# A fused Mamba-2 and SwiGLU kernel: two more value products in three parts, and a new order of the steps

## The chip, the core and the metric

The kernel runs on one core of a Trainium2 chip. The core has TensorE (PE, matrix products, with PEld loading its weights), VectorE (DVE), ScalarE (ACT), GpSimd (POOL) and SyncE (SP, which here issues nearly all transfers). Each engine has a queue of its own and runs it in order; an instruction waits by semaphores for what it needs. Products are written to PSUM, which has eight banks; all else lies in SBUF.

The metric is the device time of one execution in microseconds (us). Where a time is named below without more, it is the median of several runs.

## What is computed

A chunked state-space block (Mamba-2 SSD) with 4 batches x 8 heads, 768 tokens, head size 32 and state size 16, and behind it a SwiGLU block on the 3072 tokens with width 256 and 1536 hidden columns:

```python
# per chunk of tokens, per head
cum = np.cumsum(log_a)
L = np.exp(cum[i] - cum[j]) * (i >= j)
y = (C @ B.T * L) @ x + (C @ state) * np.exp(cum)
state = np.exp(sum(log_a)) * state + sum_j(B[j] x[j] * exp(cum[-1] - cum[j]))
# then, on x = y of all heads side by side, 3072 x 256
xn = x / np.sqrt(np.mean(x * x, -1) + 1e-6) * rms_g
g, val = xn @ w_gate, xn @ w_val          # 256 x 1536 each
out = (g / (1 + np.exp(-g)) * val) @ w_out
```

All inputs and outputs are float32.

## The kernel before

**Blocks and tiles.** The tokens are cut into 6 blocks of 512 (number blk), each of two pairs p of 256 tokens, each pair of two chunks g. The hidden columns are cut into 12 tiles f of 128. A gate product (m = 0) or value product (m = 1) of a block and a tile is one 128 x 512 result in one PSUM bank.

**Two ways to multiply.** A float32 product can be done whole (`gv_whole`, L1149, and `o_whole`): two instructions over the two halves of the 256 inner columns, which the trace shows as four records. Or it can be done in three parts (`gv_split`, L1159, and `o_split`, `product_apart`): x and w are each cut into a high part, a low part and a mixed part of the type fp32r, and six instructions add up their products. The parts have to be made first. For x these are `x_high` (the step xH on ScalarE or xHv on VectorE) and `x_part` (xL and xK on VectorE); for a weight piece k, wH or wHv, wL and wM; for a hidden tile, hH or hHv, hL (VectorE) or hLp (GpSimd), and hK. The set `GV4` holds the gate and value products that are done whole, `O4` the output products. Block 0's tiles 0 and 1 are done in another way ("early", L1112).

**Weights.** The weights come in 18 pieces, fetched by transfers (fetch), and are rebuilt from 16-bit words: ScalarE makes a power of two (pow, two instructions), VectorE a mantissa (man), and VectorE joins them (wt). Pieces 2 to 11 hold gate (even) and value (odd) columns, so the value columns of tiles 4 and 5 are piece 5; pieces 12 to 17 are the output weights.

**Order.** Nothing is scheduled by the framework. The text `order` (L1390 to L1516) lists 1200 steps, and the loop below it emits their instructions one after the other; so the text fixes the order in the queue of every engine. A step is a group (i, p or b: settings and first work, pairs, blocks), a kind and numbers. `b:X.1.10.0` is the product in three parts for block 1, tile 10, gate; `b:F.0.4.1` the whole product for block 0, tile 4, value; `b:OF` and `b:OX` are output products (whole, in parts) into one of a block's two result banks; `b:OY` are those of the last block's second half. `b:silu` (ScalarE) takes a gate product out of its bank into hx and frees the bank; `b:hid` (VectorE, L1174) multiplies the value product into hx and frees that bank.

**The state-space steps.** gb makes C B^T for a block (four banks), L multiplies it with the decays, A and S are the states, yi and ya the outputs y. The decays of a chunk are fetched (spread), the token's sum is subtracted (sub on VectorE, subp on GpSimd), the exponential taken (ex, ScalarE) and the upper triangle cut (ca on GpSimd, cav on VectorE). sq and sqa or sqav (GpSimd or VectorE), ms, rs, rb and xn are the norm. ScalarE holds one table of functions at a time: Silu has one, Exp and Ln share another, and a step that needs the other one loads it first (L264, L266; also the steps table and exps).

**Buffers.** `Ring` hands out places first in, first out: eight PSUM banks (`one`), and SBUF places h (512 columns), q, k, s and d. A step that takes a place waits for the last reader of the place that was freed longest ago.

Of the kernel before, what the change touches and what calls it, by code (L numbers as in the profile page):

```python
# [50 lines left out]
def kernel(  # L51
# [1264 lines left out]
    def token_out():  # L1316
# [98 lines left out]
        b:X.0.2.1 i:man.15 i:wH.5 i:man.14 b:table.5 b:hid.0.7 b:X.0.3.1 b:ms.1 i:fetch.17 p:qb.4  # L1415
        i:pow.11 i:pow.15 i:wM.8 i:man.11 i:wL.8 b:X.0.6.1 b:rs.1 b:hid.0.3 p:subp.10 b:X.0.9.0
        b:hid.0.5 b:X.0.8.0 i:pow.13 i:wt.11 i:wt.14 b:hid.0.6 i:pow.9 i:man.9 i:wt.15 i:man.13
        i:pow.17 p:sub.9 i:wHv.11 b:hid.0.2 i:wM.11 i:wt.9 i:wL.11 p:vB.4 p:ex.9 b:OF.0.4.0 i:man.17
        i:wH.9 i:wH.15 p:vC.4 b:OF.0.4.1 i:wt.13 b:OF.0.7.1 i:wL.9 i:wH.13 p:spread.8 b:OF.0.5.1
        i:wM.9 p:Tt.4.0 p:subp.11 p:qb.5 p:vC.5 b:rb.1 p:ex.11 b:X.0.10.0 p:x.4 i:wt.17 p:sub.8  # L1420
# [12 lines left out]
        b:OF.0.11.0 p:scale.7 p:vC.9 i:wL.4 p:scale.6 p:Tt.6.0 b:silu.1.11 b:X.1.1.0 b:table.4
        b:sq.2.1 b:put.0.0 b:hK.1.10 b:X.1.6.0 p:Tt.9.0 b:X.1.11.1 i:wL.15 b:hLp.1.0 i:wM.16
        b:X.1.6.1 b:silu.1.1 b:sq.2.0 b:hK.1.0 b:sqav.2 p:vB.6 p:dT.7 p:spread.12 b:yt.2.0 i:wM.5
        p:spread.13 b:ms.2 b:silu.1.6 i:wM.13 p:A.6 i:wL.16 p:spread.15 p:A.7 p:S.6 b:X.1.5.0
        i:wL.13 b:rs.2 b:hid.1.11 p:Tt.7.0 p:qb.10 i:wL.5 p:scale.9 p:S.7 b:exps.4 b:silu.1.5
        b:X.1.9.1 p:sub.13 b:X.1.1.1 b:X.1.4.0 b:X.1.8.1 b:exps.5 b:rb.2 b:hH.1.11 b:silu.1.4
# [6 lines left out]
        b:X.1.7.1 b:xH.2.0 b:OX.1.8.0 i:wL.14 b:X.1.3.1 b:hHv.1.4 p:yi.7 p:ya.7 p:vB.9 b:xK.2.0
        b:hK.1.1 b:xL.2.0 b:xL.2.1 b:hid.1.3 b:hH.1.2 b:hLp.1.1 b:xK.2.1 b:hLp.1.4 b:hid.1.7
        b:yt.3.0 b:hK.1.4 b:OX.1.8.1 b:hHv.1.9 b:hLp.1.6 b:X.2.2.0 b:hH.1.7 b:OX.1.1.0 p:spread.16
        b:sq.3.1 b:OX.1.4.1 b:hK.1.9 b:OX.1.4.0 b:sq.3.0 p:spread.18 p:vC.8 b:OX.1.1.1 p:x.9
        b:yt.3.1 p:dT.8 b:hL.1.2 b:hLp.1.7 b:X.2.9.0 b:sqav.3 b:hL.1.9 p:qb.8 b:X.2.0.1 b:hK.1.7
        b:X.2.2.1 b:silu.2.2 p:Tt.8.0 b:silu.2.9 p:sub.16 p:scale.11 p:vB.8 b:X.2.11.0 b:OX.1.7.0  # L1450
        p:sub.18 b:OX.1.7.1 p:x.8 b:hH.1.3 b:hK.1.2 p:scale.8 b:OX.1.9.0 b:ms.3 p:A.8 b:OX.1.2.0
        b:hK.1.3 p:S.8 b:hid.2.2 p:spread.17 b:hL.1.3 p:vC.11 p:ex.16 p:subp.17 b:X.2.7.0 b:X.2.5.0
        b:silu.2.11 b:hHv.1.5 p:Tt.8.1 p:Td.8 b:hK.1.6 p:cav.16 p:spread.19 b:X.2.0.0 b:hL.1.5
        b:X.2.5.1 b:silu.2.0 b:OX.1.9.1 b:silu.2.5 p:vB.10 p:qc.10 b:OX.1.3.1 b:hid.2.5 b:rs.3
        p:dT.11 p:qb.11 b:hH.2.5 b:hid.2.0 p:ex.17 p:ex.18 b:X.2.8.0 p:subp.19 b:hK.1.5 p:ca.18
        p:Tt.11.1 b:X.2.11.1 p:dT.9 b:OX.1.6.1 b:hLp.2.5 p:ex.19 b:X.2.4.0 b:rb.3 b:OX.1.6.0
# [98 lines left out]
```

## Time and profile before

| | us |
|---|---|
| median of 3 runs | 364.84 (364.15 to 364.86) |
| the profiled execution | 364.29 |
| its span, first to last instruction | 362.5 |
| TensorE busy | 356.3 |
| VectorE busy | 275.3 |
| ScalarE busy | 183.9 |
| GpSimd busy | 74.8 |

Where the output products of the blocks and the three parts of the gate and value products stand among the costliest groups:

```profile
L1159 PE MATMUL gv<-xh,wh 128*128 128x512 f32 x264 | 84.8, 402 | 0.0
L1159 PE MATMUL gv<-xl,wp 128*128 128x512 f32 x264 | 81.5, 390 | 0.0
L1159 PE MATMUL gv<-xk,wp 128*128 128x512 f32 x264 | 81.4, 389 | 0.0
```

Such a row gives the line, the engine, the operation, what is written and read, the shapes and the count; then the busy time of the group in us and the mean length of one in ns; then the idle time of the engine just ahead of the group's instructions and what ended it. Products overlap in TensorE, so the mean length of a record is more than the step from one to the next. A row of the timeline or of the chain begins with the start and the length in us, counted from the first instruction. A row of waits names the engine, what it was about to do, whom it waited for, the total in us, the number and the longest. "issue" is time for which the trace shows no cause.

### The profile page before, as it was taken

How to read it: one execution, taken by the hardware profiler on the slowest of the kernel's cores; microseconds unless marked ns; L12 is line 12 of the kernel's file. 1: busy time of each engine (PE TensorE's matmuls, PEld its weight loads, DVE VectorE, ACT ScalarE, POOL GpSimd, SP SyncE). 2: the span in 40 equal slices, each digit the busy share in tenths (PEclk: the TensorE clock that was granted, in tenths of full speed). 3: DMA queues.
4: the chain of work that ended last, by engine and by line, in shares of the span. 5: the costliest groups of instructions: out<-in, count | busy, mean ns of one | idle time of the engine just before them, and what ended most of it. 6: DMA issues, size and time to landing. Idle time of an engine off the chain costs nothing.

```text
span 362.5 us, 8200 instructions
## 1 busy us (share of the span) xinstructions
PE 356.3 (98%) x3301; PEld 284.0 (78%) x3301; DVE 275.3 (76%) x514; ACT 183.9 (51%) x323; POOL 74.8 (21%) x79
## 2 busy tenths in 40 slices
PE   8999989999999999999999999999999999999996
PEld 5667467888787888788788788788788888888886
DVE  6899998999999999872787884696457446629591
ACT  3879878697288946563236755225811121231110
POOL 4022004124011036212102626010010000511140
PEclk9999999999999999999999999999999999999999
DMA  8889968367525224423302031200101000100004
GB/s 103 187 140 288 272 193 224 107 151 117 103 85 137 44 40 103 103 54 85 60 12 81 7 88 31 45 0 4 36 0 31 1 0 2 29 0 2 0 7 110
DMA packets 94702, 27.95 MB, mean 77 GB/s; under 512 B 77545, under 2 KB 92617, under 8 KB 94665
## 3 DMA queue, kind: packets, MB, share of 16 engines
q1 hardware_dynamic: 92584, 27.30, 32.8%
q8 instruction: 26, 0.43, 0.5%
q10 hardware_dynamic: 2080, 0.13, 0.4%
q14 instruction: 12, 0.09, 0.1%
HBM read 23.68 MB, written 3.74 MB: 76 GB/s over the span
## 4 chain that ended last, share of the span: by engine, by line
PE 95%; DVE 2%; issue 1%; POOL 1%; ACT 0%; POOLq 0%; DVEq 0%
PE gv L1159 50%; PE o L1228 18%; PE o L1234 7%; PE gv L1149 4%; PE y L916 3%; PE o L1206 2%; PE gv L1112 2%; PE g L765 2%; PE A L830 1%; PE g L758 1%; PE y L891 1%; PE e L609 1%; POOL hl L1080 1%; PE ms L1014 0%; DVE hk L1082 0%
## 5 line engine op out<-in xcount | busy, mean ns | idle before, releaser
L1159 PE MATMUL gv<-xh,wh 128*128 128x512 f32 x264 | 84.8, 402 | 0.0
L1159 PE MATMUL gv<-xl,wp 128*128 128x512 f32 x264 | 81.5, 390 | 0.0
L1159 PE MATMUL gv<-xk,wp 128*128 128x512 f32 x264 | 81.4, 389 | 0.0
L272 ACT ACTIVATE hx<-gv 128x512 f32<-128x512 f32 x70 | 40.1, 595 | 75.3 <-PE gv L1159 36.5
L1080 POOL TENSOR_TENSOR hl<-hx,hh 128x512 fp32r<-128x512 f32 x27 | 39.5, 1473 | 172.4 <-PE o L1228 105.8
L1174 DVE SCALAR_TENSOR_TENSOR hx<-gv,hx 128x512 f32<-128x512 f32 x70 | 46.6, 683 | 26.9 <-PE gv L1159 19.3
L1159 PEld LDWEIGHTS gv<-xl,wp 128*128 128x128 f32 x264 | 49.6, 188 | 10.6
L1159 PEld LDWEIGHTS gv<-xk,wp 128*128 128x128 f32 x264 | 49.6, 188 | 10.6
L1159 PEld LDWEIGHTS gv<-xh,wh 128*128 128x128 f32 x264 | 48.6, 188 | 10.5 <-issue 0.6
L1082 DVE SCALAR_TENSOR_TENSOR hk<-hx,hh 128x512 fp32r<-128x512 f32 x60 | 47.1, 792 | 8.9 <-PE o L1228 6.0
L328 ACT ACTIVATE hh<-hx 128x512 fp32r<-128x512 f32 x35 | 21.8, 629 | 43.2 <-PE o L1228 20.3
L1228 PE MATMUL o<-hh,wh 128*128 128x512 f32 x96 | 38.0, 396 | 0.0
L1228 PE MATMUL o<-hl,wp 128*128 128x512 f32 x96 | 37.4, 390 | 0.0
L1228 PE MATMUL o<-hk,wp 128*128 128x512 f32 x96 | 37.4, 389 | 0.0
L1080 DVE TENSOR_TENSOR hl<-hx,hh 128x512 fp32r<-128x512 f32 x33 | 24.1, 744 | 5.3 <-PE o L1228 3.7
L631 POOL TENSOR_SCALAR_AFFINE_SELECT L<-L 64x512 f32<-64x512 f32 (+1 forms) x22 | 18.7, 851 | 45.8 <-ACT L L272 45.0
L322 DVE SCALAR_TENSOR_TENSOR wp<-wh,w 128x512 fp32r<-128x512 f32 x36 | 26.3, 756 | 1.0 <-ACT wh L328 1.0
L1234 PE MATMUL o<-w,hx 128*128 128x256 f32 x96 | 23.0, 381 | 0.0
L1228 PEld LDWEIGHTS o<-hh,wh 128*128 128x128 f32 x96 | 18.0, 188 | 4.3 <-issue 0.4
L1228 PEld LDWEIGHTS o<-hk,wp 128*128 128x128 f32 x96 | 18.0, 188 | 3.8
L1228 PEld LDWEIGHTS o<-hl,wp 128*128 128x128 f32 x96 | 18.0, 188 | 3.5
L1234 PEld LDWEIGHTS o<-w,hx 128*128 128x128 f32 x96 | 18.0, 189 | 3.4 <-issue 0.4
(180 smaller groups left out, 504.3 us busy)
## 6 DMA issues: line engine op xcount, KB each, us to landing
L<-rowd SPq DMA_DIRECT2D x32, 128.0 KB
x<-in_x_dram SPq DMA_DIRECT2D x24, 128.0 KB
wr<-in_moe_w_out_dram SPq DMA_DIRECT2D x6, 511.5 KB
wr<-in_moe_w_gate_dram SPq DMA_DIRECT2D x5, 511.5 KB
wr<-in_moe_w_val_dram SPq DMA_DIRECT2D x5, 511.5 KB
out_dram<-ob SPq DMA_DIRECT2D x32, 64.0 KB
bc<-in_B_dram SPq DMA_DIRECT2D x23, 64.0 KB
bc<-in_C_dram SPq DMA_DIRECT2D x23, 64.0 KB
```

The costliest lines, as they stand in the source:

```text
L272: nc.scalar.activation(**operands)
L322: nc.vector.scalar_tensor_tensor(out=(low_parts, mixed_parts)[i][k], in0=high_parts[k], scalar=(-UP, GAIN)[i], in1=view(ws[k], shape), op0 ...
L328: nc.scalar.activation(out=out, in_=in_, func=AF.Copy, scale=scale)
L631: nc.gpsimd.affine_select(out=L[r], in_=L[r], pattern=[[0, L.shape[1]], [1, HC]], compare_op=ALU.is_ge, fill=0.0, base=0, channel_multipli ...
L916: nc.tensor.matmul(out=o[first:first + n, (p % 2 * 2 + i) * HC:(p % 2 * 2 + i + 1) * HC], start=not groups & opened, stop=True, skip_group ...
L1080: engine.tensor_tensor(out=out, in0=v, in1=high, op=ALU.subtract)
L1082: nc.vector.scalar_tensor_tensor(out=out, in0=v, scalar=REST, in1=high, op0=ALU.mult, op1=ALU.subtract)
L1149: nc.tensor.matmul(out=o, lhsT=view(ws[k], fetched[k][2])[:, t, f % 2 * P:][:, 0:P], rhs=xn[:, t], start=(t == 0), stop=(t == 1))
L1159: nc.tensor.matmul(out=o, lhsT=weights_of(m, t, f)[part], rhs=view(x, [P, TB], F32R), start=(part == t == 0), stop=(part == 2 and t == 1))
L1174: nc.vector.scalar_tensor_tensor(out=v, in0=o, scalar=gain(blk, f), in1=v, op0=ALU.mult, op1=ALU.mult)
L1228: nc.tensor.matmul(out=o, lhsT=w[:, b * P:(b + 1) * P], rhs=v, start=opens, stop=True, skip_group_check=True)
L1234: nc.tensor.matmul(out=o[:, j * DM:(j + 1) * DM], lhsT=v[:, tk], rhs=w, start=opens, stop=True, skip_group_check=True)
```

## The change

`GV4` loses (0, 4, 1) and (0, 5, 1): the value products of block 0's tiles 4 and 5 are done in three parts. So the steps F.0.4.1 and F.0.5.1 become X.0.4.1 and X.0.5.1. By the functions above, the hidden tiles (0, 4) and (0, 5) get another constant factor in `hid` (`gain`), the places of xH, xL, xK of block 0 and of weight piece 5 get other counts of uses, and nothing else is computed differently.

The first 150 of the 1200 steps stay as they are. All others stand in a new order. In it some steps change their form, which moves them from one engine to another; in all:

| kind | before | after | engine |
|---|---|---|---|
| F / X | 8 / 132 | 6 / 134 | TensorE |
| hH / hHv | 35 / 25 | 30 / 30 | ScalarE / VectorE |
| xH / xHv | 9 / 3 | 7 / 5 | ScalarE / VectorE |
| wH / wHv | 10 / 8 | 9 / 9 | ScalarE / VectorE |
| hL / hLp | 33 / 27 | 27 / 33 | VectorE / GpSimd |
| sub / subp | 9 / 7 | 4 / 12 | VectorE / GpSimd |
| sqav / sqa | 4 / 1 | 1 / 4 | VectorE / GpSimd |

The diff, cut to the set, the steps up to the products that change, and the end:

```diff
-    GV4 = {(0, 2, 0), (0, 3, 0), (0, 4, 0), (0, 4, 1), (0, 5, 0), (0, 5, 1), (0, 6, 0), (0, 7, 0)}
+    GV4 = {(0, 2, 0), (0, 3, 0), (0, 4, 0), (0, 5, 0), (0, 6, 0), (0, 7, 0)}
...
-        i:early.1.0 i:norm.0 p:Tt.2.0 p:T.3 p:Tt.3.1 i:wHv.2 b:xH.0.0 i:man.5 p:Tt.3.0 i:wL.2
-        b:F.0.2.0 p:scale.3 i:early.1.1 p:scale.2 i:norm.1 i:ca.2 b:gb.1 b:exps.2 b:L.1.1 i:man.4
-        b:L.1.2 b:L.1.3 i:silu.0 i:fetch.10 b:L.1.0 i:man.3 i:gains b:xK.0.0 i:pow.4 i:pow.5
-        b:F.0.6.0 b:F.0.7.0 i:silu.1 b:silu.0.7 i:man.12 i:wt.4 b:F.0.3.0 i:pow.3 p:Td.3 p:A.2
-        i:wt.5 i:hid.1 b:silu.0.2 b:silu.0.6 i:wt.3 p:A.3 b:F.0.5.0 p:S.2 i:pow.12 i:pow.10
-        i:fetch.9 i:fetch.7 i:fetch.14 b:F.0.4.0 p:S.3 b:xHv.0.1 i:wt.12 p:yi.2 i:man.10 p:ya.2
-        p:yi.3 b:silu.0.5 i:man.8 i:wt.10 p:ya.3 i:pow.7 i:man.7 b:silu.0.4 i:hid.0 p:qc.4
-        p:spread.11 i:wHv.3 i:fetch.15 i:wt.7 i:pow.8 b:F.0.4.1 b:OF.0.1.0 b:silu.0.3 b:sq.1.1
-        i:wHv.10 b:yt.1.1 b:xL.0.0 i:wM.3 i:fetch.11 b:yt.1.0 p:spread.10 b:OF.0.0.1 i:wt.8 b:xL.0.1
-        b:OF.0.0.0 i:wL.10 i:wM.10 b:xK.0.1 p:spread.9 b:OF.0.1.1 b:sq.1.0 i:wH.7 b:F.0.5.1 i:wL.7
-        p:qc.5 i:wM.7 b:X.0.11.0 b:sqa.1 i:wL.3 i:pow.14 b:hid.0.4 b:X.0.7.1 i:wHv.8 i:fetch.13
...
-        b:OX.5.5.0 b:OY.4.1 b:OX.5.11.0 b:OY.2.1 b:OX.5.2.0 b:OY.11.0 b:OY.5.0 b:OY.1.1 b:OY.4.0
-        b:OY.2.0 b:put.4.1 b:OY.1.0 b:putv.5.0 b:puta.1 b:putva.0
+        i:early.1.0 i:norm.0 p:Tt.2.0 p:T.3 p:Tt.3.1 i:wHv.2 i:man.4 p:Tt.3.0 i:pow.4 i:early.1.1
+        i:man.5 i:gains i:fetch.10 b:xH.0.1 i:norm.1 b:F.0.2.0 i:wt.4 b:xH.0.0 b:gb.1 p:scale.2
+        b:F.0.3.0 i:ca.2 b:L.1.0 i:pow.5 b:L.1.1 b:L.1.3 b:silu.0.2 b:F.0.7.0 b:silu.0.3 i:man.12
+        i:fetch.7 p:scale.3 i:fetch.11 p:A.2 b:L.1.2 i:wt.5 i:pow.12 b:xK.0.0 p:qb.6 i:silu.0
+        i:pow.8 p:S.2 i:pow.7 p:Td.3 p:A.3 p:qb.5 b:F.0.5.0 i:silu.1 b:F.0.4.0 p:S.3 i:man.8
+        b:xK.0.1 i:pow.10 b:F.0.6.0 i:wt.12 b:silu.0.7 i:hid.0 i:wHv.5 i:man.7 p:yi.2 i:fetch.13
+        i:wM.5 i:hid.1 p:ya.2 b:silu.0.5 i:man.10 p:yi.3 p:ya.3 b:xL.0.1 i:wt.7 b:OF.0.1.0 i:man.3
+        i:wL.5 i:fetch.9 b:sq.1.0 b:OF.0.1.1 i:wt.8 b:silu.0.4 i:pow.3 b:xL.0.0 i:wt.10 i:wHv.10
+        b:silu.0.6 b:sq.1.1 p:dT.5 b:yt.1.0 b:yt.1.1 i:fetch.14 b:OF.0.0.0 b:OF.0.0.1 i:wH.8 i:wH.1
+        i:pow.14 b:X.0.4.1 p:spread.9 i:wHv.7 i:wL.10 i:wM.10 b:X.0.5.1 i:wM.7 i:fetch.15 b:X.0.11.0
...
+        b:hLp.1.2 b:OX.1.7.0 b:ms.3 b:hLp.1.1 b:yt.3.1 p:A.8 b:hid.2.0 p:spread.17 b:hK.1.2 b:rs.3
+        b:hid.2.1 b:hK.1.3 p:sub.16 b:X.2.9.0 b:hK.1.1 p:Td.8 p:S.8 b:OX.1.9.1 p:sub.17 b:OX.1.3.1
+        p:spread.19 p:qc.10 b:OX.1.9.0 b:X.2.5.1 b:silu.2.5 p:ex.16 b:silu.2.9 p:sub.19 b:X.2.11.0
...
+        b:hH.5.8 b:hL.5.3 b:hK.5.3 b:hid.5.11 b:hH.5.1 b:X.5.9.1 b:hLp.5.8 b:X.5.2.1 b:X.5.2.0
+        b:OX.5.3.0 b:hL.4.8 b:hid.5.9 b:hK.5.8 b:OY.8.1 b:OY.8.0 b:hL.5.7 b:hHv.5.9 b:hHv.5.10
...
+        b:OX.5.2.0 b:OY.5.1 b:OY.4.1 b:OY.5.0 b:OY.2.1 b:OY.1.1 b:OY.4.0 b:putv.5.0 b:OY.2.0
+        b:puta.1 b:OY.1.0 b:putva.0
```

More of the change, by code (lines that the diff above doesn't have):

```diff
@@ L1415 @@
[L1415 to L1420, printed above, removed]
@@ L1433 @@
[L1433 to L1438, printed above, removed]
@@ L1445 @@
[L1445 to L1456, printed above, removed]
@@ new lines @@
+        p:x.4 b:hid.0.2 i:pow.16 b:OF.0.6.1 i:man.16 p:qc.8 b:hid.0.11 p:subp.8 p:ex.8 p:ex.11
+        b:xL.1.1 i:wt.16 b:OF.0.2.0 p:ca.10 p:ca.11 p:dT.4 b:hid.0.9 p:vB.4 i:pow.17 p:vC.5 i:wL.0
+        p:Tt.4.1 i:wHv.13 p:Tt.5.1 p:ca.8 b:hid.0.8 p:ca.9 b:hid.0.10 b:X.1.11.0 b:X.1.10.0 i:wt.17
+        b:OF.0.3.1 b:X.1.9.0 b:table.5 p:x.5 b:silu.1.10 p:Tt.4.0 p:Tt.5.0 b:OF.0.3.0 i:wM.4
+        b:X.1.10.1 i:wM.13 b:silu.1.9 b:OF.0.2.1 b:gb.2 p:qc.6 i:wL.1 i:wL.6 p:scale.5 b:silu.1.11
+        b:hid.1.10 b:L.2.1 b:X.1.11.1 p:Td.5 p:x.7 b:OF.0.8.0 b:OF.0.8.1 p:Td.4 i:wHv.14 b:L.2.0
@@ new lines @@
+        i:wL.17 p:sub.13 b:sq.2.0 b:hH.1.0 i:wM.14 b:sq.2.1 b:yt.2.1 i:wM.12 p:vC.6 b:sqa.2
+        b:OF.0.9.0 b:X.1.4.0 p:subp.14 b:hid.1.8 p:A.6 b:silu.1.1 p:A.7 b:ms.2 p:Tt.6.1 p:S.6
+        b:X.1.7.0 b:hLp.1.0 b:rs.2 b:X.1.2.0 p:spread.12 i:wM.15 b:silu.1.4 p:S.7 b:hHv.1.8
+        p:subp.15 b:rb.2 b:OF.0.10.1 p:ex.14 i:wL.12 p:dT.6 b:X.1.4.1 b:X.1.3.0 b:X.1.5.0 p:vB.7
+        p:Td.7 b:hid.1.4 p:scale.9 b:silu.1.2 b:hK.1.10 p:subp.12 p:Tt.8.1 p:vC.9 b:X.1.1.1
+        b:put.0.0 b:silu.1.7 b:put.0.1 p:ex.12 p:cav.14 b:X.1.6.1 b:X.1.6.0 b:hid.1.1 i:wM.17
@@ new lines @@
+        b:rb.3 b:X.2.2.0 p:vC.10 b:X.2.7.0 p:ex.17 b:silu.2.2 b:silu.2.3 b:OX.1.2.1 b:OX.1.1.1
+        b:xn.3.1 b:put.1.0 b:hL.2.11 b:silu.2.8 b:hH.2.9 b:silu.2.7 b:xn.3.0 b:table.4 b:X.2.8.1
+        b:X.2.7.1 b:hid.2.3 p:dT.9 p:vB.9 b:hH.2.5 b:hK.2.1 p:cav.17 b:hid.2.8 p:qb.10 b:put.1.1
+        p:A.9 b:gb.4 p:S.9 b:X.2.2.1 b:hK.2.11 b:X.2.10.0 b:hid.2.2 b:X.2.4.1 p:Td.9 b:hLp.2.0
+        b:L.4.3 b:L.4.1 b:silu.2.4 b:L.4.2 p:Tt.10.0 b:xHv.3.1 b:hLp.2.1 p:dT.11 b:hid.2.7 p:Tt.11.1
+        b:X.2.10.1 b:hid.2.4 b:X.2.6.1 b:hHv.2.2 b:X.2.6.0 b:hLp.2.5 b:L.4.0 b:silu.2.6 p:yi.8
```

154 lines of the change are left out of this document (78 added, 76 removed).

## The prediction, made before the changed kernel ran

> **What bounds the kernel now.** I read the page first (busy shares, slices, chain by engine), then TensorE's own waits, then the chain of waits in order of time, then the load of every engine by stretch.
>
> ```profile
> span 362.5 us, 8200 instructions
> PE 356.3 (98%) x3301; PEld 284.0 (78%) x3301; DVE 275.3 (76%) x514; ACT 183.9 (51%) x323; POOL 74.8 (21%) x79
> PE   8999989999999999999999999999999999999996
> PEclk9999999999999999999999999999999999999999
> ...
> PE 95%; DVE 2%; issue 1%; POOL 1%; ACT 0%; POOLq 0%; DVEq 0%
> ```
>
> TensorE is busy in every slice, at the full granted clock, and carries 95% of the chain. The kernel is bound by the sum of its products. Whatever another engine saves is worth nothing unless TensorE waited for it, and these are all the waits of TensorE that the trace lists:
>
> ```profile
> PE y L916 <- issue: 1.3, 1, 1.3
> PE idle L434 <- DVE warm L476: 1.1, 1, 1.1
> PE o L1206 <- POOL hl L1080: 0.3, 1, 0.3
> ```
>
> The 1.1 us lies at the start, ahead of step 150, and doesn't move. So a new order can win at most 1.3 + 0.3 = 1.6 us from waits. It can lose much more: every wait that it brings in adds its whole length.
>
> ```profile
> 35.62 5.35 PE gv L1149 x12
> 40.97 0.72 PE A L830 x49
> ...
> 45.32 1.14 PE y L916 x80
> 46.46 1.30 issue
> ...
> 54.61 1.72 PE gv L1149 x4
> 56.33 5.46 PE gv L1159 x24
> ...
> 352.60 1.58 PE o L1206 x11
> ...
> 359.32 0.42 DVE ob L1216
> ```
>
> L1149 is the whole product (F), L1159 the product in three parts (X). The chain runs from one to the other without a hole except at 46.46. After 359.32 only the last copy and store are left, about 3.2 us that both orders end with.
>
> ```profile
> 30.00:50.00 20.00, 18.70 (x343) 10.71 (x342) 19.05 (x46) 16.04 (x27) 2.17 (x2) 1.00 0.92 264
> 50.00:140.00 90.00, 90.00 (x987) 72.22 (x986) 87.28 (x160) 66.66 (x114) 20.99 (x19) 1.00 0.48 111
> 140.00:160.00 20.00, 20.00 (x118) 16.12 (x117) 18.20 (x32) 11.85 (x23) 4.86 (x4) 1.00 0.45 101
> 160.00:340.00 180.00, 180.00 (x1370) 147.58 (x1369) 112.82 (x190) 66.40 (x115) 34.22 (x30) 1.00 0.12 27
> ```
>
> The columns are the stretch, its length, then busy time of PE, weight loads, VectorE, ScalarE and GpSimd. VectorE is a second bound from 30 to 140 us: it has only 90.00 - 87.28 = 2.72 us free between 50 and 140. Behind 160 it has 67 us free in 180. So the early part is where a new order can fail, and late in the kernel a step has to be badly placed to be felt.
>
> **The two products.** A whole product is four records in 1.72 us (the row at 54.61). A product in three parts is six records; 24 records took 5.46 us, so one is 5.46 / 4 = 1.365 us. Two of them changed: 2 x (1.72 - 1.365) = 0.71 us less on TensorE. All three parts of weight piece 5 and of block 0's x are made in the old order too, for other products, so no new instruction makes an operand; they are only due sooner. I count -0.71 us in full, because TensorE is the chain at that place. The factor that the two hidden tiles now carry is an immediate of an instruction that runs anyway: 0.
>
> **Are the operands there?** The first product in parts was X.0.11.0, behind eight F; now it is X.0.4.1, behind six. TensorE reaches it 2 x 1.72 = 3.44 us sooner. VectorE's queue is what must keep up:
>
> ```profile
> 49.81 0.41 DVE L331 TENSOR_SCALAR wh<-w 128x512 fp32r<-128x512 f32 x1
> 50.13 0.68 DVE L1080 TENSOR_TENSOR xl<-xn,xh 128x512 fp32r<-128x512 f32 x1
> ...
> 51.34 0.74 DVE L306 SCALAR_TENSOR_TENSOR w<-w,e 128x512 int16<-128x512 int16 x1
> 51.97 0.68 DVE L1080 TENSOR_TENSOR xl<-xn,xh 128x512 fp32r<-128x512 f32 x1
> 52.56 1.29 DVE L322 SCALAR_TENSOR_TENSOR wp<-wh,w 128x512 fp32r<-128x512 f32 x2
> 53.77 0.68 DVE L1082 SCALAR_TENSOR_TENSOR xk<-xn,xh 128x512 fp32r<-128x512 f32 x1
> ```
>
> The last operand before (xK.0.1, the row at 53.77) was done at 54.45 and the product began at 56.33: 1.88 us in hand. From start to start, a part costs (53.77 - 52.56) / 2 = 0.60, a high part 50.13 - 49.81 = 0.32, a weight's upper half 51.97 - 51.34 = 0.63. I went through VectorE's steps from number 150 to the last operand in both orders. No longer ahead of it are wL.2, wM.3, wL.10, wM.10 (4 x 0.60), wt.3 and wt.10 (2 x 0.63), xHv.0.1, wHv.3, wHv.10 (3 x 0.32): 4.62 us. New ahead of it are wHv.5, wL.5, wM.5: 1.52 us. VectorE is there 3.10 us sooner, TensorE 3.44 us: 1.88 - 0.34 = 1.54 us in hand. That hides the move, at no cost. Bounds: if the 1.30 us at 46.46 goes away TensorE comes sooner still, with 0.24 us in hand; at the other end VectorE has 19.05 of 20 busy there, so at most 0.95 us could be gained by packing it better, and a loss of 1 us needs VectorE 2.5 us late. I take 0.
>
> **The stall at 46.46** has no engine behind it: 80 and more tiny products in 1.14 us, and then TensorE had nothing to issue, while the DMA share was 0.92 (first of the stretch rows). I read it as the instruction stream arriving late. The same ten groups of products precede it in the new order, so it should fall at the same product; but the A products (40.97) now stand one F sooner, and three F instead of two (1.72 us more) lie between them and the y products, where few instructions are used up. Bounds: 0 (it stays) and -1.30 (it goes). The DMA load is unchanged in kind, the fetches are only in another order: I take 0.
>
> **Work moved between engines**, counted over both orders: `sub` to `subp` 5 times, `sqav` to `sqa` 3, `hL` to `hLp` 6 (VectorE to GpSimd), `hH`, `xH`, `wH` to the form with v 5, 2 and 1 times (ScalarE to VectorE).
>
> ```profile
> L1080 POOL TENSOR_TENSOR hl<-hx,hh 128x512 fp32r<-128x512 f32 x27 | 39.5, 1473 | 172.4 <-PE o L1228 105.8 <-PE o L1234 18.8 <-ACT hh L328 13.6
> L1080 DVE TENSOR_TENSOR hl<-hx,hh 128x512 fp32r<-128x512 f32 x33 | 24.1, 744 | 5.3 <-PE o L1228 3.7 <-POOL hl L1080 1.2
> L659 POOL TENSOR_TENSOR L<-L,tok 128x512 f32<-128x512 f32 x7 | 8.3, 1198 | 21.2 <-DMA L<-rowd 17.7 <-DMA bc<-in_B_dram 3.4
> L659 DVE TENSOR_TENSOR L<-L,tok 128x512 f32<-128x512 f32 x9 | 7.6, 854 | 0.0
> L974 DVE TENSOR_TENSOR sq<-sq 128x512 f32<-128x512 f32 x4 | 2.7, 684 | 2.6 <-ACT sq L272 2.6
> L331 DVE TENSOR_SCALAR hh<-hx 128x512 fp32r<-128x512 f32 x25 | 11.5, 468 | 8.1 <-PE o L1228 3.7 <-PE o L1234 3.4 <-PE gv L1159 0.5
> L266 ACT ACT_TABLE_LOAD x14 | 18.0, 1283 | 1.0 <-PEq L1539 0.8
> ```
>
> VectorE loses 5 x 0.854 + 3 x 0.684 + 6 x 0.744 = 10.8 us and gets 8 x 0.468 = 3.7: 7.0 us less. GpSimd gets some 18.6 us on its 74.8 (sqa is put at 1.27 us from the one that runs there, by the same view). Following the switches between Silu and Exp/Ln through both lists gives 28 table loads before and 34 after: 6 x 1.28 = 7.7 us more ScalarE, which stands at 51%; where they cluster (around rs.3 to ex.17, the stretch 140 to 160) it had 20 - 11.85 = 8.1 us free for four more. All of this is beside TensorE: 0. If that cover is gone, the price is below.
>
> GpSimd's work does slow VectorE:
>
> ```profile
> 349.00 0.69 DVE L1082 SCALAR_TENSOR_TENSOR hk<-hx,hh 128x512 fp32r<-128x512 f32 x1
> 350.81 3.44 POOL L1080 TENSOR_TENSOR hl<-hx,hh 128x512 fp32r<-128x512 f32 x2
> 351.95 1.14 DVE L1082 SCALAR_TENSOR_TENSOR hk<-hx,hh 128x512 fp32r<-128x512 f32 x1
> ```
>
> The same operation took 0.69 us, and 1.14 beside GpSimd's: 0.45 more. Between 50 and 140 us I count six more GpSimd operations in the new order (four `subp`, one `sqa`, one `hLp`), which take 4 x 0.854 + 0.684 = 4.1 us from VectorE, while three more high parts bring 3 x 0.468 = 1.4. With 6 x 0.45 = 2.7 us of slowing the balance is zero, and 2.72 us are free: 0. Here the Trainium skill speaks against the change: "SBUF — State Buffer", section "Who interferes with whom", says that a VectorE operation with two SBUF inputs and a GpSimd operation that reads SBUF exclude each other for a whole instruction. Its sum would be that of the third rival below; the 0.45 us of this trace is less than a whole one.
>
> **The end.** The old order's last X (X.5.2.1) has 10.3 us of output products behind it, counted with 0.36 us for an OY, 0.71 for an OX; the new one's (X.5.2.0) has 17.1. Its chain (hid, high part, parts) has 7 us more time, and `hL.5.2` moves from GpSimd to VectorE, so the 0.3 us wait should go: -0.33. Bounds: -0.33, and +1.5 (one `hLp` late, four of them now stand in a row). I take -0.33.
>
> **The sum**: -0.71 - 0.33 = -1.04 us. Span 362.5 becomes 361.5; the profiled execution, 364.29 with 1.8 us around its span, 363.25. It lay 0.55 us under the median of the runs, 364.84, and on that scale it is 363.8.
>
> **Rivals.**
>
> 1. *The stall at 46.46 goes.* For it: the longer stretch of F ahead of the burst. Against: the same boundary, the same loaded DMA. 363.8 - 1.3 = 362.5.
>
> 2. *PSUM banks are handed over too late.* A product takes the bank that was freed longest ago. In the old order 6 such steps stand right behind the step that frees their bank, in the new one 9 (X.1.1.0 behind hid.1.0, X.1.7.0 behind S.6, X.2.4.1 behind hid.2.2 and others).
>
> ```profile
> L1174 DVE SCALAR_TENSOR_TENSOR hx<-gv,hx 128x512 f32<-128x512 f32 x70 | 46.6, 683 | 26.9 <-PE gv L1159 19.3
> ```
>
> Each can cost up to one such operation, 0.68 us. Against: none of the six cost a listed wait. With two in nine it is 363.8 + 1.4 = 365.2.
>
> 3. *GpSimd blocks VectorE for its whole length* (the slower side). Place: 50 to 140 us, above all the four `subp` of block 2. Six operations are 4 x 1.198 + 1.473 + 1.27 = 7.5 us, against 4.1 off and 1.4 on: VectorE needs 4.8 us more and has 2.72: TensorE waits 2.1 us, 363.8 + 2.1 = 365.9. It decides from 2.72 us on, and more GpSimd work late in the order falls where VectorE is free. Against: 0.45 us measured.
>
> 4. *It doesn't do what it says*: the 0.71 us turns into waits for parts at X.0.4.1 and X.0.5.1, and the end's wait comes back elsewhere: 364.8.
>
> **Chances.** Forecast 0.42, own range 363.2 to 364.5; rivals 0.12, 0.22, 0.19, 0.05. A measurement of this kernel can tell about 0.2%, 0.73 us, from no change: faster means under 364.11, slower over 365.57. Faster: 0.32 of the forecast and all of the first rival, 0.44. Same: 0.10 of the forecast, 0.09 of the second, 0.03 of the last, 0.22. Slower: 0.13 of the second, the third, 0.02 of the last, 0.34. The range 362.3 to 366.6 reaches from just under the first rival to 0.7 us over the third, half of the bound at the end.
>
> **What would show it.** Right: X.0.4.1's six records at 0.23 us a step with no idle time ahead; TensorE's busy time about 0.7 us lower; VectorE some 7 us lower, GpSimd 18 higher; no TensorE wait between 60 and 350 us; the first row of TensorE's waits again "y from issue" with 1.3. Rival 1 shows as that row missing; rival 2 as TensorE waits on hx, S or yt between 100 and 290 us; rival 3 as VectorE full between 50 and 140, its two-input means well over 0.8 us, and TensorE waiting for VectorE there. I would be wrong altogether if a load of weights or of L were late: then TensorE or VectorE waits for a DMA.

## The result, and the profile after

The changed kernel takes 367.93 us (median of 6 runs, 366.24 to 369.5), the kernel before beside it 364.23 us (6 runs, 364.07 to 364.86). The ratio is 1.0099, with a 95% interval of 1.0070 to 1.0127: 3.7 us slower. In a later measurement it was 1.0117 (1.0091 to 1.0144).

The page of the changed kernel, in the lines that answer to those of before:

```profile
span 366.2 us, 8229 instructions
PE 357.8 (98%) x3305; PEld 284.5 (78%) x3305; DVE 279.2 (76%) x508; ACT 186.8 (51%) x321; POOL 93.6 (26%) x93
PE   8999999999998999999999999998999999999996
PEclk9999999999999999999999999999999999999999
...
PE 75%; DVE 12%; SPq 6%; DMA 3%; issue 2%; ACT 0%; DVEq 0%
```

GpSimd got 18.8 us more (74.8 to 93.6), where 18.6 were counted. VectorE's busy time did not fall by 7 us; it rose by 3.9. The chain that ended last lies on TensorE for 75% of the span instead of 95%: VectorE, SyncE's queue and a transfer have come into it. TensorE's busy time is no guide here, since the ends of products are modelled. Its listed waits are:

```profile
PE gv L1159 <- DVE xl L1080: 1.3, 1, 1.3
PE idle L434 <- DVE warm L476: 1.1, 1, 1.1
PE A L830 <- DVE hx L1174: 1.1, 1, 1.1
PE A L830 <- DMA x<-in_x_dram: 0.5, 1, 0.5
PE o L1234 <- DVE hk L1082: 0.3, 1, 0.3
PE o L1234 <- DVE w L306: 0.3, 1, 0.3
PE gv L1159 <- DVE wp L322: 0.2, 1, 0.2
```

The stall "y from issue" of 1.3 us is gone, and five waits for VectorE and one for a transfer are new. To find all of the loss, I took from both traces the time from each product's start to the next one's and subtracted the median for the same pair of kinds. What is over that median is time that TensorE lost (the time given is the start of the product ahead of the loss):

| stretch, us | before | after | what is new |
|---|---|---|---|
| 0 to 20 | 4.16 | 4.37 | |
| 20 to 60 | 4.89 | 4.28 | 1.50 at 46.2 gone; 0.75 + 0.27 at A.3, 39.6 to 40.7 |
| 60 to 80 | 1.06 | 2.08 | 0.28 + 0.41 + 0.44 at 62.2, 66.1 and 67.1 |
| 80 to 100 | 2.02 | 2.13 | |
| 100 to 120 | 1.24 | 2.94 | 1.30 inside A.7, at 110.6 |
| 120 to 240 | 4.26 | 4.64 | |
| 240 to 260 | 0.88 | 2.52 | 1.52 at X.4.7.0, 250.6 |
| behind 260 | 0.66 | 0.67 | 0.45 at 357 for 0.49 at 352 |

The sum is 19.17 before and 23.63 after: 4.46 us more, less the 0.71 us of the two products is 3.75, and the spans differ by 3.7. So the loss sits at three places, 62 to 67, 111 and 250 us, and each is a wait for VectorE. Two more are the exchange in the early part: the stall that is gone, and a wait on a transfer at 40 us. Here are that transfer, as the chain shows it, and TensorE's rows in the timeline at the four places (start, length, and in brackets the idle time ahead with what ended it):

```profile
36.62 4.09 DMA x<-in_x_dram
```

```profile
40.34 0.76 PE L830 MATMUL A<-x,Bd 64*32 64x64 f32 x32 [0.54 <-DMA x<-in_x_dram]
...
66.77 0.73 PE L1159 MATMUL gv<-xk,wp 128*128 128x512 f32 x2 [0.25 <-DVE wp L322]
67.77 1.13 PE L1234 MATMUL o<-w,hx 128*128 128x256 f32 x4 [0.27 <-DVE w L306]
...
111.86 0.43 PE L830 MATMUL A<-x,Bd 64*32 64x64 f32 x24 [1.09 <-DVE hx L1174]
...
252.32 0.50 PE L1159 MATMUL gv<-xl,wp 128*128 128x512 f32 x1 [1.35 <-DVE xl L1080]
```

Why is VectorE late there? Its rows and GpSimd's rows at the three places:

```profile
60.20 1.60 DVE L300 TENSOR_SCALAR w<-wr 128x512 f32<-128x512 uint32 x2
62.55 1.26 DVE L300 TENSOR_SCALAR w<-wr 128x512 f32<-128x512 uint32 x1
...
106.91 1.77 DVE L659 TENSOR_TENSOR L<-L,tok 128x512 f32<-128x512 f32 x1
...
247.62 1.77 DVE L1082 SCALAR_TENSOR_TENSOR xk<-yt,xh 128x512 fp32r<-128x512 f32 x1
249.31 1.76 DVE L1082 SCALAR_TENSOR_TENSOR hk<-hx,hh 128x512 fp32r<-128x512 f32 x1
```

```profile
58.69 2.49 POOL L659 TENSOR_TENSOR L<-L,tok 128x512 f32<-128x512 f32 x2 [4.56 <-DMA L<-rowd]
62.44 1.09 POOL L659 TENSOR_TENSOR L<-L,tok 128x512 f32<-128x512 f32 x1 [1.26 <-DMA L<-rowd]
...
106.48 1.66 POOL L974 TENSOR_TENSOR sq<-sq 128x512 f32<-128x512 f32 x1 [2.44 <-ACT sq L272]
...
247.46 3.06 POOL L1080 TENSOR_TENSOR hl<-hx,hh 128x512 fp32r<-128x512 f32 x2 [5.80 <-PE o L1228]
```

Alone these VectorE operations take 0.42 (L300) or 0.68 us. Beside GpSimd one of them ends only some 0.5 us (L300: 0.3) after GpSimd's instruction has ended: 106.48 + 1.66 = 108.14, and the operation that began at 106.91 ends at 108.68. That is a hold until GpSimd is through, not a slowing. The form of the low part shows it in its mean, which was 744 ns before:

```profile
L1080 DVE TENSOR_TENSOR hl<-hx,hh 128x512 fp32r<-128x512 f32 x27 | 22.6, 836 | 10.1 <-PE o L1228 9.8 <-PE gv L1159 0.2
```

I counted every VectorE operation behind the first 23 us that overlaps a GpSimd one and is over 0.2 us longer than the median of its form. Before, 26 are held, for 18.1 us in all; after, 38, for 27.3 us; none for more than 1.15 us. One held operation loses 0.7 us on average in both, where 0.45 was predicted. The sum grew at all three places: from 2.0 to 3.2 us between 50 and 70, 1.6 to 4.1 between 90 and 115, 0 to 3.5 between 240 and 260. It also grew from 2.7 to 5.8 between 140 and 180, and from 2.0 to 4.1 behind 330, where TensorE waited hardly longer than before, and it fell from 4.7 to 2.6 between 180 and 240: a hold costs only where a product stands close behind it. The 9.2 us more are not simply the price of the 14 operations that moved. By the same count e1 below, the new order with as few GpSimd instructions as before (79), still has 34 held, for 25.8 us: how much is held depends on the order too.

### The profile page after: what moved, and what is told of

Read it like the earlier page. It is cut to its first block, busy times and chain, and to the rows that moved or that the text cites. A ratio compares the mean times of both kernels' runs of the same rounds, so it can differ in the third digit from the quotient of the medians.

```text
span 366.2 us, 8229 instructions
## 1 busy us (share of the span) xinstructions
PE 357.8 (98%) x3305; PEld 284.5 (78%) x3305; DVE 279.2 (76%) x508; ACT 186.8 (51%) x321; POOL 93.6 (26%) x93
## 4 chain that ended last, share of the span: by engine, by line
PE 75%; DVE 12%; SPq 6%; DMA 3%; issue 2%; ACT 0%; DVEq 0%
PE gv L1159 46%; PE o L1228 17%; PE o L1234 5%; SPq L160 3%; DVE wp L322 2%; DVE hk L1082 2%; PE y L916 2%; SPq L205 2%; SPq L241 2%; PE gv L1149 1%; PE o L1206 1%; DMA x<-in_x_dram 1%; DMA rowd<-r_sb 1%; DVE hx L1174 1%; DVE w L300 1%
## 5 line engine op out<-in xcount | busy, mean ns | idle before, releaser
L1080 POOL TENSOR_TENSOR hl<-hx,hh 128x512 fp32r<-128x512 f32 x33 | 48.4, 1475 | 172.2 <-PE o L1228 69.1
L1159 PE MATMUL gv<-xh,wh 128*128 128x512 f32 x268 | 86.3, 403 | 0.0
L1159 PE MATMUL gv<-xl,wp 128*128 128x512 f32 x268 | 83.1, 391 | 1.3 <-DVE xl L1080 1.3
L1159 PE MATMUL gv<-xk,wp 128*128 128x512 f32 x268 | 82.7, 390 | 0.2 <-DVE wp L322 0.2
L1174 DVE SCALAR_TENSOR_TENSOR hx<-gv,hx 128x512 f32<-128x512 f32 x70 | 47.2, 684 | 40.2 <-PE gv L1159 32.2
L1159 PEld LDWEIGHTS gv<-xh,wh 128*128 128x128 f32 x268 | 49.4, 188 | 11.3 <-issue 1.3
L1082 DVE SCALAR_TENSOR_TENSOR hk<-hx,hh 128x512 fp32r<-128x512 f32 x60 | 48.6, 826 | 9.4 <-PE gv L1159 3.4
L328 ACT ACTIVATE hh<-hx 128x512 fp32r<-128x512 f32 x30 | 18.7, 631 | 30.7 <-DVE hx L1174 11.0
L1080 DVE TENSOR_TENSOR hl<-hx,hh 128x512 fp32r<-128x512 f32 x27 | 22.6, 836 | 10.1 <-PE o L1228 9.8
L322 DVE SCALAR_TENSOR_TENSOR wp<-wh,w 128x512 fp32r<-128x512 f32 x36 | 27.5, 792 | 0.0
L631 POOL TENSOR_SCALAR_AFFINE_SELECT L<-L 64x512 f32<-64x512 f32 (+1 forms) x22 | 17.9, 812 | 28.5 <-ACT L L272 27.6
```

The lines of the kernel that those rows point to most:

```text
L322: nc.vector.scalar_tensor_tensor(out=(low_parts, mixed_parts)[i][k], in0=high_parts[k], scalar=(-UP, GAIN)[i], in1=view(ws[k], shape), op0 ...
L328: nc.scalar.activation(out=out, in_=in_, func=AF.Copy, scale=scale)
L631: nc.gpsimd.affine_select(out=L[r], in_=L[r], pattern=[[0, L.shape[1]], [1, HC]], compare_op=ALU.is_ge, fill=0.0, base=0, channel_multipli ...
L1080: engine.tensor_tensor(out=out, in0=v, in1=high, op=ALU.subtract)
L1082: nc.vector.scalar_tensor_tensor(out=out, in0=v, scalar=REST, in1=high, op0=ALU.mult, op1=ALU.subtract)
L1159: nc.tensor.matmul(out=o, lhsT=weights_of(m, t, f)[part], rhs=view(x, [P, TB], F32R), start=(part == t == 0), stop=(part == 2 and t == 1))
```

## The experiments

The early part varies from run to run (see e14 and the last section). So beside the ratio I give **the rest**: the time from the first product behind block 1's y products to the end of the last product, in the profiled execution. Before it is 310.04 us, after 314.24, in a second profile of the changed kernel 314.03. It holds the same work, less 0.71 us after. It is one execution of each kernel, and a kernel that is late early finds more operands ready behind (see e10), so it is read together with the ratio. These rows begin it, before and after:

```profile
49.18 1.55 PE L1149 MATMUL gv<-xn,w 128*128 128x512 f32 x3
```

```profile
48.76 3.72 PE L1234 MATMUL o<-w,hx 128*128 128x256 f32 x16
```

| run | median, us | ratio to before (95%) | rest, us |
|---|---|---|---|
| changed kernel | 367.93 | 1.0099 (1.0070 to 1.0127) | 314.24 |
| e1 old forms | 375.78 | 1.0299 (1.0271 to 1.0328) | 320.87 |
| e2 xL.4.1 earlier | 367.99 | 1.0092 (1.0063 to 1.0121) | 313.15 |
| e3 two hL on VectorE | 366.82 | 1.0044 (1.0024 to 1.0064) | 313.08 |
| e4 hid.1.8 earlier | 367.05 | 1.0062 (1.0035 to 1.0088) | 313.28 |
| e5 F ahead of A | 368.59 | 1.0094 (1.0068 to 1.0120) | 314.09 |
| e6 three sub on VectorE | 369.59 | 1.0108 (1.0066 to 1.0151) | 316.44 |
| e7 four repairs | 366.08 | 1.0028 (1.0011 to 1.0046) | 312.32 |
| e8 new to 290, then old | 367.88 | 1.0082 (1.0053 to 1.0110) | 313.22 |
| e9 five places | 365.66 | 1.0014 (0.9995 to 1.0034) | 310.88 |
| e10 order at 62 | 369.39 | 1.0104 (1.0077 to 1.0131) | 312.94 |
| e11 two whole again | 370.15 | 1.0124 (1.0084 to 1.0164) | 315.15 |
| e12 old behind 736 | 365.83 | 1.0028 (1.0014 to 1.0042) | 311.03 |
| e13 e9 and F ahead of A | 365.75 | 1.0034 (1.0016 to 1.0052) | 311.14 |
| e14 old order, A earlier | 365.09 | 1.0006 (0.9986 to 1.0027) | 310.06 |
| e15 changed kernel again | 369.14 | 1.0117 (1.0091 to 1.0144) | 314.03 |
| e16 e12 and F ahead of A | 365.80 | 1.0020 (1.0000 to 1.0040) | 311.51 |

**e1: is it GpSimd's larger share as such?** All 88 steps that change their form go back to the old one, in the new order.

```diff
-... p:subp.9 ... p:subp.8 ... i:wHv.13 ... b:hLp.1.10 ... b:sqa.2 ...
+... p:sub.9 ... p:sub.8 ... i:wH.13 ... b:hL.1.10 ... b:sqav.2 ...
```

> The new order, with every step in the form (and so on the engine) that it had in the old order; 14 operations of GpSimd go back to VectorE, which pays 10.8 - 3.7 = 7.1 us for the forms. Theory A, GpSimd holds VectorE up and the forms are the cause: about 14 x 1 us of holding goes, the four TensorE waits of the changed kernel (39.6, 62 to 67, 110.6 and 250.6 us) shrink to the first one, and the time falls by 3 to 4 us to 364 or 365. Theory B, the places in the order are the cause, and the forms only add to it: holding goes, but VectorE's own work grows by half as much, the waits move to other places, and the time stays within 1.5 us of 367.9.

Its ratio is 1.0299, some 7 us worse than the changed kernel's. Neither theory foretold that: A said 3 to 4 us less, B no more than 1.5 us away. TensorE waits in places of its own:

```profile
PE gv L1159 <- DVE L L788: 1.8, 1, 1.8
PE o L1206 <- DVE hl L1080: 1.7, 1, 1.7
PE gv L1159 <- DVE xl L1080: 1.6, 2, 1.3
PE o L1234 <- DVE hx L1138: 1.2, 1, 1.2
```

By its forms VectorE has 7.1 us more work of its own here, and the run does not tell this apart from the holds that stayed (25.8 us). What it does show is that taking GpSimd's larger share back does not win the loss back: with its instructions at 79 again the new order is slower still. So the places were taken one by one.

**e2 and e3: the wait at 250 us, repaired by place and by form.**

```diff
-b:hK.3.9 ... b:xK.4.0 ... b:hK.3.5 b:hid.3.4 ... b:xL.4.1
+b:xL.4.1 b:hK.3.9 ... b:xK.4.0 ... b:hK.3.5 b:hid.3.4 ...
```

> The changed kernel with one step moved: the low part of the second half of block 4's x stands ahead of hK.3.9, four VectorE steps sooner. If TensorE's wait of 1.3 us at 250.6 us (1.52 more than the usual step) is one of place, it goes and nothing takes its place: 1.3 to 1.5 us less, 366.4 to 366.6. If VectorE is late there with everything, the wait only moves to the next operand (xK or hK) and the time stays at 367.9.

```diff
-b:xL.4.1 b:hLp.3.10 b:hH.3.1 b:X.4.7.0 b:hLp.3.5
+b:xL.4.1 b:hL.3.10 b:hH.3.1 b:X.4.7.0 b:hL.3.5
```

> The changed kernel with hL.3.10 and hL.3.5 on VectorE instead of GpSimd, in the same places of the order, which are behind the late step xL.4.1. If GpSimd's two instructions at 247.46 us are what held the two VectorE operations there (1.77 and 1.76 us instead of 0.68), these are 0.68 again, xL.4.1 comes 2.2 us sooner and the whole wait of 1.3 us goes: 366.4 to 366.6. If one GpSimd instruction costs VectorE 0.45 us, as predicted, xL.4.1 comes 0.9 us sooner and 0.4 us of wait stays: 367.0. If something else slows VectorE there, the two stay at 1.7 us and the time at 367.9.

VectorE's rows there, of e2 and then of e3:

```profile
247.75 0.68 DVE L1080 TENSOR_TENSOR xl<-yt,xh 128x512 fp32r<-128x512 f32 x1
248.35 1.77 DVE L1082 SCALAR_TENSOR_TENSOR hk<-hx,hh 128x512 fp32r<-128x512 f32 x1
250.04 1.76 DVE L1082 SCALAR_TENSOR_TENSOR xk<-yt,xh 128x512 fp32r<-128x512 f32 x1
```

```profile
249.03 0.68 DVE L1082 SCALAR_TENSOR_TENSOR xk<-yt,xh 128x512 fp32r<-128x512 f32 x1
249.63 0.68 DVE L1082 SCALAR_TENSOR_TENSOR hk<-hx,hh 128x512 fp32r<-128x512 f32 x1
```

With GpSimd's two instructions taken away the operations are 0.68 us again, 1.09 less each, and no wait is left at 250 us: the rest is 1.16 us shorter and the ratio falls from 1.0099 to 1.0044, outside the changed kernel's interval. At this place the hold is shown. In e2 the two holds stay and only fall on other steps, so its second expectation holds in part; TensorE still loses 0.64 us at the next product, and the rest is 1.09 shorter. Its ratio hardly fell (1.0092), and its early part was 1.2 us longer than in the changed kernel's profile. Both steps that held VectorE stand *behind* xL.4.1 in the order: GpSimd's queue runs on by itself, so a step there acts earlier than its place says.

**e4: the bank that A.7 waits for.**

```diff
-p:sub.13 ... p:subp.14 b:hid.1.8 p:A.6 b:silu.1.1 p:A.7
+b:hid.1.8 p:sub.13 ... p:subp.14 p:A.6 b:silu.1.1 p:A.7
```

> The changed kernel with hid.1.8, which frees the bank that A.7 waits for, moved ahead of sub.13, so past three VectorE operations that took 1.77 and 2 x 1.06 us beside GpSimd's. If the wait of 1.1 us at 111 us (1.30 more than the usual step) is the late handing over of that one bank, it goes and the time falls by 1.1 to 1.3 us to 366.7. If VectorE is simply full there, TensorE waits for the next thing, S.6 or a part of weight pieces 14, 16 or 17, and the time stays at 367.9.

The wait in A.7 goes; a shorter one comes at X.1.7.0, whose bank S.6 frees:

```profile
110.72 0.89 PE L830 MATMUL A<-x,Bd 64*32 64x64 f32 x64
...
112.33 0.73 PE L1159 MATMUL gv<-xh,wh 128*128 128x512 f32 x2 [0.36 <-DVE A L847]
```

The rest is 0.96 shorter, and the ratio falls to 1.0062, though its interval still overlaps the changed kernel's: between the two expectations, nearer to the first. No run takes away the GpSimd instructions at 103 to 110 us alone. That their holds (1.09, 1.09 and 0.84 us on three operations of VectorE ahead of hid.1.8) make the bank late is argued from their size.

**e5: the transfer at 40 us.**

```diff
-p:A.2 b:L.1.2 ... p:A.3 b:F.0.5.0
+b:F.0.5.0 p:A.2 b:L.1.2 ... p:A.3
```

> The changed kernel with F.0.5.0 ahead of A.2 and A.3, so that four whole products stand ahead of them as in the old order. If the wait of A.3 at 39.6 to 40.7 us is the transfer x.3 that lands then, it goes: 1.0 us less, 366.9. If instead TensorE may not come to the small y products sooner than it does, because the stall of 1.5 us that the old order had at 46.24 us comes back as soon as TensorE is early, then the wait at 40 goes, the stall stands at 46 again, and the time stays at 367.9.

The wait on x.3 goes, and the stall is back:

```profile
PE y L916 <- issue: 0.9, 1, 0.9
```

TensorE is through with the y products at 48.72 us, and was at 48.76 with the wait. The time stays, as the second expectation said. In all 18 traces one of the two stands and never both: the wait on x.3 where at most three F stand ahead of A.3, the stall where four do. So they act as one loss in two places; why TensorE stalls at 46 us no run shows.

**e6 and e10: 62 to 67 us, by form and by place.**

```diff
-p:subp.11 ... p:subp.9 ... p:subp.10
+p:sub.11 ... p:sub.9 ... p:sub.10
```

> The changed kernel with sub.9, sub.10 and sub.11 on VectorE, in their places of the order, which are behind the late steps wt.14, wM.3 and wt.15. If the three GpSimd instructions at 58.7 to 63.5 us are what makes these late (three VectorE operations there take 1.12, 1.26 and 1.26 us instead of 0.68 and 0.42), the waits of TensorE at 62.2, 66.1 and 67.1 us (0.28 + 0.41 + 0.44 over the usual step) go: 1.1 us less, 366.8, if the 3 x 0.85 us that VectorE then has to do find room before 110 us; if they find none, the bank at 111 us comes later by as much, and the time is 368 or above.

```diff
-i:wM.8 i:man.9 ... i:wt.11 b:OF.0.5.0 i:wM.3 i:man.13 ... i:wt.15
+i:wM.8 ... b:OF.0.5.0 i:wM.3 i:man.9 i:man.13 ... i:wt.15 i:wt.11
```

> The changed kernel with only wt.11 and man.9 moved behind wt.15 and wM.3. If the place of these steps is what matters, the three waits at 62 to 67 us go without more work for VectorE: 366.8. If VectorE is the bound up to 115 us, what is won at 62 is waited for at 70 to 111 us: 367.9.

From the start of OF.0.1.0 to that of OF.0.7.1 the changed kernel takes 19.01 us, e6 17.69: the three waits, 1.32 us, are gone. In e6 the operations that were held run at their own length:

```profile
59.58 0.68 DVE L322 SCALAR_TENSOR_TENSOR wp<-wh,w 128x512 fp32r<-128x512 f32 x1
60.18 0.76 DVE L300 TENSOR_SCALAR w<-wr 128x512 f32<-128x512 uint32 x2
...
61.69 0.41 DVE L300 TENSOR_SCALAR w<-wr 128x512 f32<-128x512 uint32 x1
```

But then VectorE has the subtractions to do itself, and there is no room for them before 115 us: TensorE loses 1.12 us at 79, where it lost none, and 1.73 instead of 1.30 at 111, together more than it won. Behind the wait at 111 the granted clock fell to 0.5 for 3.41 us in this profile (last section); that is up to 1.7 of the 2.2 us by which the rest is longer.

e10 takes 17.69 us too, but that is not its edit alone. Its early part was 51.4 us long instead of 48.8, and in e15, where the unchanged kernel came there just as late (51.5), the stretch took 17.96: TensorE came late and found its operands ready. At like times of arrival the edit is worth 0.3 to 0.7 us there: 17.69 beside those 17.96, and 18.01 in e9, which holds it, beside 18.69 in e3, which does not (both came at 49.7). With GpSimd's three subtractions gone all of the 1.32 us goes, whenever TensorE comes (e6 at 49.1, e7 at 48.7: 17.69 and 17.84). So at 62 to 67 us too it is the hold that is shown, and the place of man.9 and wt.11 is worth part of it. Beside e15 the rest of e10 (312.94) is 1.09 us shorter, 0.45 of it at 111 us. The ratio shows no gain (1.0104); in three of its six executions the granted clock was 0.994 or 0.995, as in the profiled one (last section).

**e7 and e9: several places at once.** e7 joins e3, e4, e5 and e6. e9 joins e3, e4 and e10, and:

```diff
-p:S.6 b:X.1.7.0 ... b:OF.0.10.1
+p:S.6 b:OF.0.10.1 b:X.1.7.0 ...
...
-b:put.4.1 b:hK.5.1
+b:hK.5.1 b:put.4.1
```

> The changed kernel with four repairs at once: hL.3.10 and hL.3.5 on VectorE, hid.1.8 ahead of sub.13, F.0.5.0 ahead of A.2, and sub.9 to sub.11 on VectorE. If the four waits are the whole loss and don't depend on one another: 367.9 - 1.5 - 1.3 - 1.0 - 1.1 = 363.0, under the kernel before. If a wait that is removed only brings TensorE to the next late operand, less than half of it is won: 365.5 or above.

> The changed kernel with repairs that give VectorE no more work early: wt.11 and man.9 stand behind wt.15 and wM.3 (the waits at 62 to 67 us, 1.13 us), hid.1.8 ahead of sub.13 (1.30 at 111) with OF.0.10.1 between S.6 and X.1.7.0, hL.3.10 and hL.3.5 on VectorE (1.52 at 250.6), hK.5.1 ahead of put.4.1 (0.45 at 357). If VectorE's lateness at these places is the whole loss: 367.9 - 4.4 = 363.5, under the kernel before by 0.9. If half of each is found again at the next operand: 365.7.

e7 wins 1.9 us of the rest, less than half of what it hoped for, as its second expectation said: it holds the subtractions of e6, and 1.16 us come back at 79. e9 wins 3.4 us of the rest (310.88), and its listed waits are short:

```profile
PE idle L434 <- DVE warm L476: 1.1, 1, 1.1
PE A L830 <- DVE A L847: 0.8, 1, 0.8
PE o L1228 <- DVE hk L1082: 0.2, 1, 0.2
PE o L1234 <- DVE hk L1082: 0.2, 1, 0.2
```

(The second is the wait of A.3 on x.3, here under the name of a VectorE operation that ended close by.) Of a ratio of 1.0099, 1.0014 is left, which can't be told from none. This shows VectorE's lateness at single places to be most of the loss: 3.4 of the 4.2 us by which the rest had grown, with nearly as much GpSimd work as in the changed kernel (91 instructions instead of 93). Some 1.0 of it lies between 60 and 80 us, where e9 also came 1.0 us later than the changed kernel. The first expectation, 0.9 us under the kernel before, is not met: it is 365.66 beside 365.15. What is left, 0.84 us and the 0.71 of the two products, is by the count above some 1.0 us between 120 and 240 us and 0.3 between 100 and 120, in small waits that no run takes apart.

**e11: are the two products worth 0.71 us?**

```diff
-b:X.0.4.1 ... b:X.0.5.1
+b:F.0.4.1 ... b:F.0.5.1
```

> The changed kernel with the value products of block 0's tiles 4 and 5 done whole again, in the places where the new order has them; the order is the new one. If TensorE is the bound at that place, as the prediction counted, its 0.71 us come back in full: 368.6. If VectorE is the bound between 52 and 67 us, TensorE only waits less at 62 to 67 us and the time stays at 367.9: then the two products in three parts were worth nothing in this order.

From OF.0.1.0 to X.0.9.0 it takes 13.05 us against 12.32: 0.73 more, as counted. At OF.0.7.1, behind the three waits, only 0.09 is left beside the changed kernel, and 0.41 beside e3, which began that stretch at the same time (49.7 us): VectorE sets the pace there. By the end the rest is 0.91 longer, but part of that is a wait at 111 us that is 0.43 longer, and e3 and e15, which do the two products in three parts, have this longer wait as well. The ratios, 1.0124 and 1.0099, have intervals that overlap. The price of the products is right; what it comes to in this order stays open.

**e8, e12, e13, e16: a better version?** e8 and e12 take the new order up to step 290 or 736 (e12 with e9's repairs there) and the old order and forms behind; e13 and e16 add e5's move to e9 and e12.

> The new order up to its step 290 (about 67 us), with the two products in three parts, and behind it the remaining steps in the old order and the old forms. If the new order wins early (0.71 us by the products, 1.5 us by the stall at 46 us, less about 1.0 us at 40 and 1.1 us at 62 to 67) and loses all of the rest behind 100 us, the time is 364.0 to 364.6, that of the kernel before. If the old order behind the joint is as late with its operands as the new one, because the joint leaves VectorE behind, 366 or above.

> The new order with the repairs of e9 up to its step 736 (about 180 us), and behind it the remaining steps in the old order and the old forms. If what is left of the loss in e9 (1.4 us of small waits against the old order, of which 0.3 stand between 180 and 200 us) is spread over both halves, the time is 0.3 to 0.7 us under e9, at that of the kernel before: 364.2 to 365.0 where the kernel before has 364.3 to 365.1. If the 0.71 us of the two products come out whole, it is 0.2% under the kernel before. If the joint leaves a part late, 366 or above.

> e9, and F.0.5.0 ahead of A.2 and A.3 as in e5. If standing on the transfer x.3 costs the new order about 1 us in most executions (in the profiles so far TensorE is through with the y products of block 1 at 48.8 to 51.4 us where A.3 comes first, at 48.7 in both where F.0.5.0 does), the time is 0.5 to 1.0 us under e9 and at or under the kernel before: a ratio of 0.998 to 1.000. If the wait only changes its place (to the stall at 46 us), it is that of e9, a ratio of 1.001 to 1.002.

> e12, and F.0.5.0 ahead of A.2 and A.3. If A.3's place costs 1 us, 0.5 to 1.0 us under e12: a ratio to the kernel before of 0.999 to 1.001. If it only changes its place, 1.003 as e12.

e8 missed in its first expectation, and its second (366 or above) came true: right behind the joint TensorE waits 0.8 us for a weight's part and 1.1 for a rebuilt weight, which the joint leaves late. e12, e13 and e16 end where e9 does, 0.14 to 0.34% over the kernel before; the gains that were hoped for in each did not come. So the old half behind 180 us gives nothing that e9 did not have, and A.3's place does not matter to the median. None beats the kernel before.

**e14 and e15: the early part.** e14 does to the old order what the new one does to A.

```diff
-b:F.0.3.0 ... p:A.2 ... p:A.3
+p:A.2 ... p:A.3 b:F.0.3.0
```

> The kernel before with one step moved: F.0.3.0 stands behind A.2 and A.3, so that three whole products stand ahead of these as in the new order. If the place of A.3 costs the new order time, the old one gets the wait on x.3 (1 to 1.8 us at 40 us), loses its stall at 46 us (1.5), and is 0 to 1 us slower, with a wider spread of its runs. If the stall is independent of the wait, both stand in its profile and it is 1.0 us slower or more.

> The changed kernel itself once more, beside the others: 367.2 to 368.6. Its profile shows the waits at 62 to 67, 111 and 250 us again; by both theories the wait of A.3 at 40 us is between 1.0 and 2.0 us.

e14 is not slower than the kernel before (1.0006), though in its profile, the slowest of its 12 executions, TensorE waited 2.0 us at A.3 and had no stall at 46. So the early exchange is not the loss. e15 has the waits at 111 and 250 again (1.5 and 1.3), those at 62 to 67 hardly: it came there 2.8 us later. Its median, 369.14 us, lies over the 368.6 that were expected.

## Why the prediction was wrong, point by point

The forecast was 363.8 us and a range up to 366.6; it is 367.93, and slower where faster had the largest chance.

- **The two products, -0.71**: made where they stand (0.73 measured). Behind the next waits for VectorE 0.09 to 0.41 of it was left; what lasts to the end is open (e11).
- **The operands in time, 0**: right. X.0.4.1 began without a wait, its six records 0.23 us apart but for the first step. Its last operand (xL.0.0, on VectorE from 50.23 us for 0.70) was done 1.20 us before, where 1.54 were forecast:

```profile
52.13 0.81 PE L1159 MATMUL gv<-xh,wh 128*128 128x512 f32 x2
52.78 0.62 PE L1159 MATMUL gv<-xl,wp 128*128 128x512 f32 x2
53.24 0.61 PE L1159 MATMUL gv<-xk,wp 128*128 128x512 f32 x2
```

- **The stall at 46.46, 0**: it went, by 1.5 us, but the first rival's 1.3 us were not won: A.3, one F sooner, stood before a transfer that lands near 40.7 us and paid 1.0. Together 0.6 us from 20 to 60. The prediction saw A move and did not ask when x.3 lands, though it named a wait on a transfer (of weights or of L) as what would make it wrong.
- **Work moved between engines, 0: the step that failed.** "With 6 x 0.45 = 2.7 us of slowing the balance is zero, and 2.72 us are free". As a balance this came out nearly right. Between 50 and 140 us the holds grew from 6.1 to 9.4 us, some 3.3 where 2.7 were counted, and VectorE has 90.00 - 87.26 = 2.74 us free after the change, as it had 2.72 before:

```profile
50.00:140.00 90.00, 88.27 (x921) 70.76 (x920) 87.26 (x156) 61.14 (x103) 26.39 (x23) 1.00 0.46 104
```

What is wrong is to conclude 0 from it. TensorE meets one operand or one bank at a time, and there it met 1.1 us (62 to 67) and 1.3 us (111) of waits with those 2.74 us free elsewhere. The size is wrong in the same way: 0.45 was one row, while the 26 holds of that same trace average 0.7 us and reach 1.15. Two holds of 1.09 us in a row ahead of xL.4.1 made it 2.2 us late and TensorE waited 1.3 of them.
- **"Behind 160 us a step has to be badly placed to be felt"**: xL.4.1 was one, with 67 us free around it. It cost 1.5 us, and e3 shows GpSimd behind it.
- **The end, -0.33**: not made. Three hLp in a row held three VectorE operations by about 1 us each, and the wait of 0.3 us stayed.
- **The rivals**: the third was right that GpSimd blocks VectorE for a whole instruction, and gave 365.9. Its 2.1 us came from the same kind of balance, with VectorE full between 50 and 140 us. It was not full, so it is luck that 1.1 + 1.3 us were lost there; and the 1.5 us at 250 us it left out, since VectorE is free there. The Trainium skill ("SBUF — State Buffer", "Who interferes with whom") says that the later of the two blocks until the first is through; the trace agrees (106.91 to 108.68 beside 106.48 to 108.14), and the row of 0.45 us was a hold that began late. The second rival's sign came too: A.7 waits 1.1 us on hx for its bank, more than the 0.68 us of one operation, as VectorE was held ahead of that hid. X.1.7.0, which the rival named, got its bank late only where hid.1.8 stands earlier (0.36 us in e4).
